# Where the group sums and the gate batches live, and the order of the first loads

## The chip, the core and the metric

The kernel runs on one core of a Trainium2 chip. Its time is the device time of one launch in microseconds; the time before is the median of 15 runs, 952.01 us (951.11 to 956.47). Engines are called as the profile calls them: PE multiplies matrices, DVE and ACT work on vectors, POOL and SP here do little but start transfers.

## What is computed

A linear attention block without softmax, with an RMS norm, feeds a two-layer MLP whose gate is h * erf(softplus(h)):

```python
kv = np.einsum('bhsd,bhse->bhde', k, v)            # q, k, v: 8 x 8 x 576 x 64, float32
out = np.einsum('bhsd,bhde->bhse', q, kv)
rms = np.sqrt(np.mean(out * out, axis=-1, keepdims=True) + 1e-06)
x = out / rms * g_norm                             # then heads side by side: 4608 x 512
h = x @ w_in                                       # w_in 512 x 2048, w_out 2048 x 512, float64
sp = np.maximum(h, 0.0) + np.log1p(np.exp(-np.abs(h)))
y = (h * erf(sp)) @ w_out                          # 4608 x 512
```

## The kernel before, in words

**Groups and batches.** The 4608 tokens are nine groups T of 512: the first 512 tokens of each of the 8 sequences, and a ninth group of their last 64 tokens each. Within a group the 2048 features are 16 chunks f of 128, in batches of 4. Attention works on pairs p of heads, four to a group: `products` (k-transposed times v, and transposes of q), `apply`, `mean` and `norm` make one quarter of a group's input x.

**Weights.** They arrive as float64. `load_w` brings raw words, `w_split` and `w_join` rebuild float32 from exponent and mantissa on DVE and ACT. During group 1 they are also cut into three reduced-precision parts (`w_upper`, `w_lower`) and written back to DRAM, from where `load_parts` fetches them over and over for groups 2 to 8.

**Groups 0 and 1** (the loop over n, L666 to L763) compute mostly with plain float32 matmuls (h_ps L713, o_ps L534). The sums over features stay in four PSUM banks o_ps and are copied out by `sums` (L553). For group 1 this is done after 12 of its 16 chunks; its last batch goes on into the main loop.

**The main loop** (m from 8 to 36, L808 to L881) does a batch per turn. `hidden` makes n_ps and m_ps for each of 4 chunks (8 and 4 matmuls); ACT copies n_ps into h (L856), DVE adds m_ps (L459), ACT takes softplus (L858) and erf (L862), DVE multiplies (L876). Then `result` multiplies the batch before, m - 1, with w_out for four token blocks j and adds into the sums e: for a group's first batch DVE writes e (L797), later it adds (L454), each time followed by the add of m_ps (L459). In a group's last batch each block is stored (L545) as soon as it is summed. So the stores of group 1 are issued in m = 8, and the first sums of group 2 are written in m = 9; the stores of group 2 come in m = 12, the first sums of group 3 in m = 13. Pieces of attention for the next group are put between.

**Tiles.** The pool `wide` (L90) has two buffers of 128 x 4 x 512 floats under one tag, taken in turns: by x of group 0, x of group 1, x_high and x_both (parts of group 1's x), the sums of group 1, and then by h of each batch from m = 8 on. So h of m = 8 follows x_both, and h of m = 9 follows the sums of group 1. The pool `acc` (L672) has one such buffer: the sums of group 0, then `old_h` (h of group 1's last batch, m = 7), then the sums of each group from 2 on (L795). An instruction that writes a reused buffer waits for the last users of the tile before it, stores among them.

**The start.** `load_part` (L120) loads one of q, k, v of a pair: q has 128 partitions with pieces of 256 bytes (256 KB), k and v 96 partitions with 1536 bytes (288 KB each). A list written by hand (L157 to L168) names, in the order of issue, the loads of pairs 0 to 2 and the engine whose queue takes each (SP or ACT). The last 64 tokens of q (`load_last`, 32 KB a pair) go over POOL, after it has made the identity and cleared bd_kv, followed by g_norm. Then SP issues two raw weight loads and pair 3, then more weights and pairs 4 and 5. The hardware queues share eight completion semaphores, so an issue waits for the landing of the eighth issue before it. `keep_warm` (L582) issues matmuls whose result nobody reads: 8 before the first pair and 4 after the first pair's products. The order of all instructions is as written (`manual_schedule`).

Of the kernel before, what the change touches and what calls it, by code (L numbers as in the profile page):

```python
# [39 lines left out]
FP32 = mybir.dt.float32  # L40
FP32R = mybir.dt.float32r
# [9 lines left out]
BATCH = 4  # L51
# [3 lines left out]
FIRST = 2  # L55
# [5 lines left out]
def kernel(  # L61
# [25 lines left out]
    attp = ctx.enter_context(tc.tile_pool(name="attp", bufs=1))  # L87
    dram = ctx.enter_context(tc.tile_pool(name="dram", bufs=1, space=bass.MemoryType.DRAM))

    wide = ctx.enter_context(tc.tile_pool(name="wide", bufs=2, side="right"))  # L90

    room, early_room, low_room = (ctx.enter_context(ExitStack()) for _ in range(3))
    first_w = room.enter_context(tc.tile_pool(name="first_w", bufs=1, side="right"))
# [23 lines left out]

        return 6 if T == 0 else 5

    def load_part(i, name, side=nc.sync):  # L120
        T, p = divmod(i, NP)
        pool = early if i in (2, 3) else kvp
        if name == "q":
            t = q_sb[T, p] = pool.tile([P, J, 2, D], FP32, name="q_sb", tag="q")
            side.dma_start(
                out=t, in_=q[T, 2 * p : 2 * p + 2, 0:G, :].rearrange("h (p j) d -> p j h d", j=J)
            )
        else:
            got, src = (k_sb, k) if name == "k" else (v_sb, v)
            C = chunks(T)  # L130
            rows, rest = divmod(S, C)
            assert rest < 2
            t = got[T, p] = pool.tile([rows + rest, 2, C, D], FP32, name=f"{name}_sb", tag=name)
            heads = src[T, 2 * p : 2 * p + 2]
            side.dma_start(
                out=t[:rows].rearrange("r h c d -> r h (c d)"),
                in_=heads[:, : S - rest].rearrange("h (r c) d -> r h (c d)", c=C),
            )
            if rest:
                side.dma_start(  # L140
                    out=t[rows:, :, 0], in_=heads[:, S - rest :].rearrange("h r d -> r h d")
                )

    def load_pair(i):
        if i < B * NP:
            for name in "qkv":
                load_part(i, name)

    def load_last(T, p, side=nc.sync):
        if T < B:  # L150
            side.dma_start(
                out=q_last[p % 2 * R : p % 2 * R + R, p // 2],
                in_=q[T, 2 * p : 2 * p + 2, G:S, :].rearrange("h r d -> r h d"),
            )


    for i, name, side in (  # L157
        (0, "k", nc.sync),
        (0, "v", nc.scalar),
        (0, "q", nc.sync),  # L160
        (1, "k", nc.scalar),
        (1, "v", nc.scalar),
        (1, "q", nc.sync),
        (2, "k", nc.sync),
        (2, "v", nc.sync),
        (2, "q", nc.sync),
    ):
        load_part(i, name, side)  # L168

    w_in_sb = first_w.tile([P, KC, DF], FP32, name="w_in_sb")  # L170
    w_out_sb = first_w.tile([P, FC, DM], FP32, name="w_out_sb")
# [1 line left out]

    ident = const.tile([P, P], FP32, name="ident")
    make_identity(nc, ident)
    bd_kv = const.tile([P, 2, P], FP32, name="bd_kv")
    nc.gpsimd.memset(bd_kv, 0.0)
    for i in range(NP):
        load_last(0, i, nc.gpsimd)
    g_col = const.tile([P, 1], FP32, name="g_col")  # L180
    for i in range(2):
        nc.gpsimd.dma_start(
            out=g_col[i * D : i * D + D, :], in_=g_norm.rearrange("(d one) -> d one", one=1)
        )
    mean_w = const.tile([P, P], FP32R, name="mean_w")
    mean_f = early.tile([P, P], FP32, name="mean_f", bufs=1)
    nc.vector.memset(mean_f, 0.0)
# [4 lines left out]
    nc.vector.memset(exp_col, -896.0 * (1 << 23))  # L192
    eps_col = const.tile([P, 1], FP32, name="eps_col")
    nc.vector.memset(eps_col, EPS)
    gm_col = const.tile([P, 1], FP32, name="gm_col")
    nc.gpsimd.tensor_scalar(out=gm_col, in0=g_col, scalar1=-0.5, scalar2=None, op0=ALU.mult)
    x_last = const.tile([P, KC, G], FP32, name="x_last")
# [85 lines left out]
    def attention(T, p, pools=None):  # L283
# [94 lines left out]
        def norm():  # L378
            ms, u, r = (st.pop(name) for name in ("ms", "u", "r"))
            nc.vector.scalar_tensor_tensor(  # L380
                out=u, in0=ms, scalar=EPS, in1=u, op0=ALU.add, op1=ALU.mult
            )
            nc.vector.scalar_tensor_tensor(
                out=u, in0=u, scalar=3.0, in1=r, op0=ALU.subtract, op1=ALU.mult
            )
            if T < FIRST:
                if T not in xT:
                    xT[T] = wide.tile([P, KC, G], FP32, name="xT", tag="h")
                x = xT[T][:, p, :]
            else:  # L390
                x = st["x"] = x_new.tile([P, G], FP32, name="x", tag="x")
            nc.vector.scalar_tensor_tensor(
                out=x,
                in0=st.pop("o"),
                scalar=gm_col,
                in1=u,
                op0=ALU.mult,
                op1=ALU.mult,
            )
# [166 lines left out]

    for _ in range(2):
        w_next("load")
    load_pair(NP - 1)

    w_rounds = {
# [4 lines left out]
        6: ("split", "join", "load", "join", "load"),  # L576
    }
    banks_0 = {"kv_ps": (ps_at, "at"), "qt_ps": (ps_h, "h"), "ms_ps": (ps_h, "h")}

    idle = ps_o.tile([P, P], FP32, name="idle", tag="o3")  # L580

    def keep_warm(n):  # L582
        for _ in range(n):
            nc.tensor.matmul(idle, lhsT=mean_w.bitcast(FP32), rhs=mean_f, start=True, stop=True)

    keep_warm(8)
    first = [attention(0, p, banks_0 | {"se_ps": (ps_o, f"o{p}")}) for p in range(NP)]
    for i in range(NP + 3):
        for piece, p in ((0, i), (1, i - 1), (4, i - 3), (3, i - 2)):
            if 0 <= p < NP:  # L590
                first[p][piece]()
        if i == 0:
            keep_warm(4)
        if i == 1:
            for _ in range(RAW - 2):
                w_next("load")
            load_pair(NP)
            load_pair(NP + 1)
        for what in w_rounds.get(i, ()):
            w_next(what)  # L600
# [65 lines left out]
    for n in range(FIRST * FC + 1):  # L666
# [23 lines left out]
            gates(done)  # L690
        if T == FIRST - 1:
            if f == 0:
                x_high = wide.tile([P, KC, G], FP32R, name="x_high", tag="h")
                x_low = low.tile([P, KC, G], FP32R, name="x_low")
                for i in range(0, KC, 2):
                    upper(xT[T][:, i : i + 2], x_high[:, i : i + 2])
                for i in range(0, KC, 2):
                    lower_only(xT[T][:, i : i + 2], x_high[:, i : i + 2], x_low[:, i : i + 2])
# [21 lines left out]
        if T < FIRST:  # L720
            if n == whole:
                old_h = acc.tile([P, BATCH, G], FP32, name="h", tag="e")
            h = hs[n] = old_h[:, n - whole] if n >= whole else unit("h_sb")
            s = ss[n] = unit("s_sb")
            if n in plain:
                nc.scalar.copy(h, plain.pop(n))
            else:
                nc.scalar.activation(h, n_ps, AF.Copy, scale=SHIFT - 1.0)
                add(h, m_ps)
            if T == FIRST - 1:  # L730
                if f == 1:
                    x_both = wide.tile([P, KC, G], FP32R, name="x_both", tag="h")
                    for i in range(0, KC, 2):
                        both_only(x_high[:, i : i + 2], x_low[:, i : i + 2], x_both[:, i : i + 2])
                    x_forms[T] = x_high, x_low, x_both
                gates(done)
                for key in list(w_new):
                    w_lower(*key)
                for key in to_cut[f]:
                    w_upper(*key)  # L740
            nc.scalar.activation(s, h, AF.Softplus)
            if n == 0:
                w_next("split")
            for piece in steps[f][1]:
                piece()
            if f % BATCH == BATCH - 1:
                for i in range(n - BATCH + 1, n + 1):
                    nc.scalar.activation(ss[i], ss[i], AF.Erf)
                softplus_table()
            if T == FIRST - 1:  # L750
                load_parts("in", {FC - 3: 2, FC - 2: 1, FC - 1: 1}.get(f, 0))
        if n >= LAG:
            T2, f2 = divmod(n - LAG, FC)
            last = n - LAG in (FC - 1, whole - 1)
            project(f2, hs[n - LAG], last)
            if last:
                sums(*((acc, "e") if T2 < FIRST - 1 else (wide, "h")))
                if T2 == 0:
                    for j in range(J):
                        store(T2, j, es.pop(j))  # L760
# [26 lines left out]
    def result(T, b, j, g, w):  # L787
# [4 lines left out]
        )  # L792
        if b == 0:
            if j == 0:
                all_e = acc.tile([P, J, DM], FP32, name="e", tag="e")  # L795
                es.update((i, all_e[:, i]) for i in range(J))
            nc.vector.tensor_scalar(  # L797
                out=es[j], in0=ps[0], scalar1=SHIFT - 1.0, scalar2=None, op0=ALU.mult
            )
        else:  # L800
            add_scaled(es[j], ps[0], SHIFT - 1.0)
# [6 lines left out]
    for m in range(first_batch, batches + 1):  # L808
# [32 lines left out]
        g, done = g_next, len(g_next)  # L841
        g_next = []
        if m < batches:
            h = wide.tile([P, BATCH, G], FP32, name="h", tag="h")
            s = gate_r.tile([P, BATCH, G], FP32, name="s", tag="s")
        for i in range(BATCH):
            if m < batches:
# [68 lines left out]
```

## Time and profile before

| | |
|---|---|
| median of 15 runs | 952.01 us |
| the profiled execution | 952.87 us, span 951.1 |
| PE busy | 932.0 us, 98% of the span |
| DVE, ACT busy | 740.9 and 616.9 us |
| DMA queues, share of 16 engines | 77.6% for SP's, 0.5% for ACT's, under 0.1% for POOL's |
| groups 0 and 1, until m = 8 begins | 255.3 us |
| 112 h copies (L856), mean | 587 ns |
| 28 first writes of sums (L797), median | 684 ns |

Times in the trace count from the start of the span. A matmul of float32 operands shows as two rows; one row of 128 x 512 in the main loop comes every 0.227 us. "Idle before" is time in which an engine had nothing running before a group of instructions, with what ended it.

### The profile page before, as it was taken

What the parts mean: (1) busy time and instruction counts of PE and PEld (TensorE: products, weight loads), DVE (VectorE), ACT (ScalarE), POOL (GpSimd) and SP (SyncE); (2) the same over time, 40 slices, a digit from 0 to 9 for tenths busy, and PEclk for the clock granted to TensorE, in tenths of its full rate; (3) what the DMA queues carried; (4) which work ended last, traced back from release to release, by engine and by line L of the source; (5) the groups of instructions that cost most, each with busy time, mean ns of one, the idle gap of its engine ahead of it and who ended that gap; (6) DMA issues with size and microseconds to landing.
All of it is one profiled execution on the core that took longest, in us unless ns stands there. A gap on an engine that the chain in (4) does not pass through costs nothing.

```text
span 951.1 us, 11799 instructions
## 1 busy us (share of the span) xinstructions
PE 932.0 (98%) x4296; PEld 687.8 (72%) x4296; DVE 740.9 (78%) x1054; ACT 616.9 (65%) x825; POOL 4.7 (0%) x14
## 2 busy tenths in 40 slices
PE   7999999999998999999999999999999999999998
PEld 5444445666686888888888888888888888878886
DVE  3979958887575888887888888888887877777667
ACT  4889876777765666666666666666666666665552
POOL 1000000000000000000000000000000000000000
PEclk9999999999999999999999999999999999999999
DMA  9856505899698888998889888988896778758872
GB/s 260 288 162 213 161 2 222 312 356 337 223 362 327 291 286 277 301 309 288 295 306 311 295 293 309 316 300 293 292 326 258 264 255 350 287 221 319 323 272 64
DMA packets 111394, 259.78 MB, mean 273 GB/s; under 512 B 43352, under 2 KB 69032, under 8 KB 111336
## 3 DMA queue, kind: packets, MB, share of 16 engines
q1 hardware_dynamic: 110200, 257.48, 77.6%
q10 hardware_dynamic: 944, 1.41, 0.5%
q8 instruction: 34, 0.56, 0.2%
q14 instruction: 24, 0.20, 0.1%
q0 software_dynamic: 192, 0.13, 0.0%
HBM read 224.40 MB, written 34.60 MB: 272 GB/s over the span
## 4 chain that ended last, share of the span: by engine, by line
PE 84%; ACT 6%; DVE 6%; DMA 2%; issue 1%; SPq 0%; DVEq 0%; ACTq 0%
PE n_ps L476 44%; PE m_ps L476 22%; PE o_ps L534 8%; PE h_ps L713 3%; PE se_ps L339 2%; PE kv_ps L311 2%; PE qt_ps L333 2%; DMA q_sb<-in_q_dram 1%; DMA w_in_parts<-w_in 1%; ACT w_e L229 1%; ACT L103 1%; DVE h L459 1%; DMA v_sb<-in_v_dram 1%; ACT w_m L233 1%; PE ms_ps L360 1%
## 5 line engine op out<-in xcount | busy, mean ns | idle before, releaser
L476 PE MATMUL n_ps<-x_forms,w_in_parts 128*128 128x512 f32 x896 | 234.3, 403 | 3.4 <-ACT h L856 1.8
L476 PE MATMUL n_ps<-w_out_parts,g_forms 128*128 128x512 f32 x928 | 231.3, 391 | 0.0
L476 PEld LDWEIGHTS n_ps<-x_forms,w_in_parts 128*128 128x128 f32 x896 | 167.7, 189 | 47.7 <-issue 9.6
L476 PEld LDWEIGHTS n_ps<-w_out_parts,g_forms 128*128 128x128 f32 x928 | 174.2, 188 | 38.4 <-issue 1.7
L858 ACT ACTIVATE s<-h 128x512 f32<-128x512 f32 x112 | 71.2, 636 | 180.9 <-DVE h L459 180.9
L459 DVE TENSOR_TENSOR h<-m_ps,h 128x512 f32<-128x512 f32 x116 | 79.9, 689 | 66.7 <-ACT h L856 48.5
L476 PE MATMUL m_ps<-w_out_parts,g_forms 128*128 128x512 f32 x464 | 124.2, 389 | 0.0
L476 PE MATMUL m_ps<-x_forms,w_in_parts 128*128 128x512 f32 x448 | 120.4, 391 | 0.0
L534 PE MATMUL o_ps<-w_out_sb,h_sb 128*128 128x512 f32 x224 | 100.8, 593 | 0.3 <-DVE h_sb L664 0.3
L476 PEld LDWEIGHTS m_ps<-w_out_parts,g_forms 128*128 128x128 f32 x464 | 87.1, 188 | 18.1
L476 PEld LDWEIGHTS m_ps<-x_forms,w_in_parts 128*128 128x128 f32 x448 | 84.2, 188 | 17.7
L459 DVE TENSOR_TENSOR e<-m_ps,e 128x512 f32<-128x512 f32 x116 | 80.3, 692 | 18.2 <-PE m_ps L476 10.9
L454 DVE SCALAR_TENSOR_TENSOR e<-n_ps,e 128x512 f32<-128x512 f32 x88 | 60.4, 686 | 38.5 <-PE n_ps L476 38.5
L534 PEld LDWEIGHTS o_ps<-w_out_sb,h_sb 128*128 128x128 f32 x224 | 42.3, 190 | 48.9 <-issue 46.6
L856 ACT ACTIVATE h<-n_ps 128x512 f32<-128x512 f32 x112 | 65.7, 587 | 11.8 <-DMA w_in_parts<-w_in 7.9
L425 DVE SCALAR_TENSOR_TENSOR g_forms<-g_forms 128x1024 fp32r<-128x1024 f32 x58 | 71.1, 1225 | 2.0
L422 DVE TENSOR_TENSOR g_forms<-h,g_forms 128x1024 fp32r<-128x1024 f32 x58 | 70.6, 1218 | 1.8 <-ACT g_forms L419 1.4
L419 ACT ACTIVATE g_forms<-h 128x1024 fp32r<-128x1024 f32 x58 | 58.9, 1061 | 13.8 <-PE m_ps L476 11.1
L876 DVE TENSOR_TENSOR h<-h,s 128x1024 f32<-128x1024 f32 x56 | 66.0, 1219 | 0.4 <-ACT s L862 0.4
L713 PE MATMUL h_ps<-xT,w_in_sb 128*128 128x512 f32 x144 | 64.9, 594 | 0.8 <-DVE w_in_sb L254 0.7
L106 ACT ACT_TABLE_LOAD x44 | 56.5, 1283 | 0.7
L862 ACT ACTIVATE s<-s 128x1024 f32<-128x1024 f32 x56 | 56.3, 1054 | 0.3
(101 smaller groups left out, 1024.4 us busy)
## 6 DMA issues: line engine op xcount, KB each, us to landing
w_out_parts<-w_out SPq DMA_DIRECT2D x116, 768.0 KB
w_in_parts<-w_in SPq DMA_DIRECT2D x112, 768.0 KB
w_in<-w_new SPq DMA_DIRECT2D x16, 768.0 KB
q_sb<-in_q_dram SPq DMA_DIRECT2D x32, 256.0 KB
w_raw<-in_moe_w_out_dram SPq DMA_DIRECT2D x8, 1024.0 KB
out_dram<-e SPq DMA_DIRECT2D x32, 256.0 KB
k_sb<-in_k_dram SPq DMA_DIRECT2D x28, 287.5 KB
v_sb<-in_v_dram SPq DMA_DIRECT2D x28, 287.5 KB
```

What stands on the lines that cost most here:

```text
L106: nc.scalar.preload_act_table_set("softplus")
L419: nc.scalar.activation(high, x, AF.Copy, scale=1.0 + 2.0**-13)
L422: nc.vector.tensor_tensor(out=low, in0=x, in1=high.bitcast(FP32), op=ALU.subtract)
L425: nc.vector.scalar_tensor_tensor(out=both, in0=low.bitcast(FP32), scalar=SHIFT, in1=high.bitcast(FP32), op0=ALU.mult, op1=ALU.add,)
L454: nc.vector.scalar_tensor_tensor(out=out_, in0=ps, scalar=scale, in1=out_, op0=ALU.mult, op1=ALU.add)
L459: nc.vector.tensor_tensor(out=out_, in0=ps, in1=out_, op=ALU.add)
L476: nc.tensor.matmul(ps, lhsT=weights(form, k), rhs=moving(form, k), start=(form == forms[0] and k == 0), stop=(form == forms[-1] and k == 3),)
L534: nc.tensor.matmul(o_ps[j], lhsT=g[:, j * P : j * P + P], rhs=w_out_sb[:, f, :], start=(f == 0), stop=last,)
L713: nc.tensor.matmul(plain[i], lhsT=w_in_sb[:, c, i % FC * P : i % FC * P + P], rhs=xT[T][:, c, :], start=(c == 0), stop=(c == KC - 1),)
L856: nc.scalar.activation(h[:, i], n_ps, AF.Copy, scale=SHIFT - 1.0)
L858: nc.scalar.activation(s[:, i], h[:, i], AF.Softplus)
L876: nc.vector.tensor_tensor(out=part(h, half), in0=part(h, half), in1=part(s, half), op=ALU.mult)
```

## The change

The group sums and the h tiles change places, and the start goes over to another order of loads without idle matmuls.

- `wide` has one buffer for each of two tags, "a" and "b". x of group 0, x_high and the sums of groups 1 to 8 take "a"; x of group 1, x_both and h of even batches m take "b"; h of odd batches takes the buffer of `acc` that the sums had.
- The loads of the start are issued pair by pair, all q on SP, k and v of pairs 0 to 2 on ACT. The last-token loads of group 0 go to SP as well: pairs 0 and 1 after the first q, pairs 2 and 3 after the first two raw weight loads. g_norm is POOL's first work.
- `keep_warm` and its PSUM tile are gone.

```diff
-    wide = ctx.enter_context(tc.tile_pool(name="wide", bufs=2, side="right"))
+    wide = ctx.enter_context(tc.tile_pool(name="wide", bufs=1, side="right"))
...
-    for i, name, side in (
-        (0, "k", nc.sync),
-        (0, "v", nc.scalar),
-        (0, "q", nc.sync),
-        (1, "k", nc.scalar),
-        (1, "v", nc.scalar),
-        (1, "q", nc.sync),
-        (2, "k", nc.sync),
-        (2, "v", nc.sync),
-        (2, "q", nc.sync),
-    ):
-        load_part(i, name, side)
...
-    for i in range(NP):
-        load_last(0, i, nc.gpsimd)
     g_col = const.tile([P, 1], FP32, name="g_col")
     for i in range(2):
         nc.gpsimd.dma_start(
             out=g_col[i * D : i * D + D, :], in_=g_norm.rearrange("(d one) -> d one", one=1)
         )
+    for i in range(NP - 1):
+        load_pair(i)
+        if i == 0:
+            load_last(0, 0)
+            load_last(0, 1)
...
+        side = nc.scalar if i < 3 else nc.sync
...
-                    xT[T] = wide.tile([P, KC, G], FP32, name="xT", tag="h")
+                    xT[T] = wide.tile([P, KC, G], FP32, name="xT", tag="ab"[T])
...
     for _ in range(2):
         w_next("load")
+    load_last(0, 2)
+    load_last(0, 3)
     load_pair(NP - 1)
...
-    keep_warm(8)
...
-        if i == 0:
-            keep_warm(4)
...
-                x_high = wide.tile([P, KC, G], FP32R, name="x_high", tag="h")
+                x_high = wide.tile([P, KC, G], FP32R, name="x_high", tag="a")
...
-                    x_both = wide.tile([P, KC, G], FP32R, name="x_both", tag="h")
+                    x_both = wide.tile([P, KC, G], FP32R, name="x_both", tag="b")
...
-                sums(*((acc, "e") if T2 < FIRST - 1 else (wide, "h")))
+                sums(*((acc, "e") if T2 < FIRST - 1 else (wide, "a")))
...
-                all_e = acc.tile([P, J, DM], FP32, name="e", tag="e")
+                all_e = wide.tile([P, J, DM], FP32, name="e", tag="a")
...
-            h = wide.tile([P, BATCH, G], FP32, name="h", tag="h")
+            pool, tag = (acc, "e") if m % 2 else (wide, "b")
+            h = pool.tile([P, BATCH, G], FP32, name="h", tag=tag)
```

In the new `load_pair` the q load of a pair always goes to SP, and `side` is the queue of its k and v.

## The prediction

> **What bounds the kernel now.** I read the page's busy shares first, then its chain of work that ended last, then the list of waits.
>
> ```profile
> PE 932.0 (98%) x4296; PEld 687.8 (72%) x4296; DVE 740.9 (78%) x1054; ACT 616.9 (65%) x825; POOL 4.7 (0%) x14
> ...
> PE 84%; ACT 6%; DVE 6%; DMA 2%; issue 1%; SPq 0%; DVEq 0%; ACTq 0%
> ```
>
> PE is busy nearly all the time and makes 84% of the chain. So only places where PE stands can be won, and a delay counts only where it makes PE stand. The list of waits (engine, line, what it waited for: total us, times, longest) has one long wait behind a DMA:
>
> ```profile
> ACT h L856 <- DMA w_in_parts<-w_in: 7.9, 1, 7.9
> ...
> PE n_ps L476 <- ACT h L856: 1.8, 1, 1.8
> ```
>
> It occurs once. What it costs is read from busy times by stretch, each stretch one batch of the main loop, cut where PE takes up n_ps<-x_forms for the next (batches m = 8 to 13; columns: length, then PE, PEld, DVE, ACT busy):
>
> ```profile
> 255.26:280.00 24.74, 24.74 (x130) 19.98 (x128) 18.67 (x28) 16.84 (x23) 0.00 (x0) 1.00 0.90 321
> 280.00:309.28 29.28, 25.93 (x130) 19.95 (x128) 19.10 (x27) 15.84 (x21) 0.00 (x0) 1.00 0.92 342
> 309.28:333.98 24.70, 24.70 (x130) 19.99 (x128) 20.16 (x30) 16.06 (x22) 0.00 (x0) 1.00 0.83 287
> 333.98:358.80 24.82, 24.82 (x131) 20.09 (x128) 20.13 (x30) 16.01 (x22) 0.00 (x0) 1.00 0.86 291
> 358.80:383.53 24.73, 24.73 (x130) 19.98 (x128) 20.28 (x30) 15.93 (x21) 0.00 (x0) 1.00 0.82 276
> 383.53:408.36 24.83, 24.83 (x131) 20.10 (x129) 20.34 (x30) 15.94 (x21) 0.00 (x0) 1.00 0.94 325
> ```
>
> Every batch takes 24.7 to 24.8 us but the second, m = 9, with 29.28. Its twin one group later is m = 13: same place in its group, same loads, 24.83. So the wait costs 29.28 - 24.83 = 4.45 us, more than PE's own 1.8, because ACT and DVE come out of it late and PE then waits for them again. The timeline shows what released ACT:
>
> ```profile
> 281.42 0.38 SPq L545 DMA_DIRECT2D out_dram<-e  x1
> ...
> 290.69 0.60 ACT L856 ACTIVATE h<-n_ps 128x512 f32<-128x512 f32 x1 [7.91 <-DMA w_in_parts<-w_in]
> ```
>
> The releaser's name is that of a load landing at the same moment. In the program the h of m = 9 takes the tile that held group 1's sums, so its first copy waits for the four stores of them; the last was issued at 281.42 and its semaphore is complete at 290.17.
>
> **The change, part by part.** The built programs' instruction orders agree on every engine but in two places: the first loads with the idle matmuls, and which waits stand in batch m = 9. DVE's order does not change at all.
>
> *The tiles.* In m = 9 ACT's first h copy and DVE's first h add lose the wait for the four stores (h now takes the tile acc "e"). DVE's first `e<-n_ps` of that batch (L797) gains it, since the sums of group 2 take the tile from which group 1's were stored. Gain of the first: 4.45 us. Price of the second: without the stall PE reaches this result as in m = 13, whose first L797 starts 397.65 - 383.53 = 14.12 us after its batch; for m = 9 that is 294.1, and the stores have landed at 290.17, 3.9 us before. The same wait already stands before L797 in groups 3 to 8 and costs nothing there; all idle time before this line is PE's:
>
> ```profile
> its engine sat idle before it (us, times) until:
>   PE n_ps L476: 11.8, 13
> ```
>
> So 0. If that cover were gone, DVE would stand, and behind it the add that frees m_ps, the gate products (L876) and the h adds, hence ACT and PE. What is late next in m = 9? Its w_in loads were issued at 258.64 (two), 270.63 and 274.67, the last is complete at 285.2 and PE wants it at about 289; of its w_out loads the last is complete at 289.5, wanted at about 292. Both hold by 2.5 us or more. Bounds of this part: -4.45 and, if all comes back, 0; I take -4.45, because the twin row shows the batch in its new state.
>
> *The first loads.* Before, SP issues k and q of pair 0, q of pair 1, k, v, q of pair 2; ACT issues v of pair 0 and k, v of pair 1; POOL the four last-token loads. Now SP has every q, with two last-token loads behind the first and two behind the first two w_raw loads; ACT has k and v of pairs 0 to 2, its last three issues waiting for landings of q of pair 0 and the first two last-token loads; POOL keeps g_norm's two. Pair 3 follows on SP in both. What counts is when pair 3 lands, because the chain of the start hangs there:
>
> ```profile
> 13.48 6.00 DMA v_sb<-in_v_dram
> 19.48 0.14 issue
> 19.62 0.92 PE kv_ps L311 x24
> ```
>
> From 20.57, when DVE copies that kv_ps, DVE's order is filled to 38 us almost without gap, then ACT's; so a later landing moves the whole rest one to one. An earlier one gains at most DVE's idle time before it since the first weights came at 14.62: 0.96 + 0.60 = 1.6 us. The bytes ahead of that landing are the same set in both orders: four pairs of q, k, v (3328 KB), four last-token loads (128), two w_raw (1024), about 4.6 MB; and the DMA engines are saturated, with 2.56 MB at 256 GB/s from 2 to 12 us and 2.48 MB at 331 from 12 to 19.5. Reordering moves bytes, it does not remove them. If all 4.6 MB went at 256, pair 3 would land at 2 + 17.9 = 19.9, that is +0.4; at the slowest 2 us slice, 239 GB/s, +1.7. I take +0.4, since q's small packets now share the engines with k and v for longer, as in that slower stretch. Bounds: -1.6 and +1.7. SP issues the last-token loads at some 0.7 us each (2.8 us in all) but gives k of pair 0 and k, v of pair 2 to ACT (0.40, 3.75 and 0.81 us), and v of pair 3 is issued 6.0 us ahead of its landing, so queues cover these. ACT's first copy (10.68) comes after its added issues; the landings they wait for (9.33 the latest before) come earlier now, so 0.
>
> *The idle matmuls.* 24 PE rows go, 12 matmuls. They do not delay anything (pair 0's kv_ps starts at 5.76 when v lands), but they bear on the clock. Granted clock by stretch (seventh number):
>
> ```profile
> 6.00:9.40 3.40, 0.86 (x24) 0.72 (x22) 0.00 (x0) 0.00 (x0) 0.00 (x0) 1.00 1.20 273
> 9.40:13.00 3.60, 3.53 (x27) 3.34 (x29) 0.73 (x3) 0.59 (x1) 0.22 (x1) 0.53 1.14 273
> 13.00:16.40 3.40, 3.40 (x52) 2.51 (x50) 1.50 (x6) 1.76 (x4) 0.00 (x0) 1.00 1.14 362
> 16.40:19.80 3.40, 2.46 (x16) 1.18 (x15) 3.20 (x9) 2.68 (x6) 0.00 (x0) 1.00 1.10 301
> 19.80:23.20 3.40, 3.40 (x35) 2.02 (x33) 2.33 (x7) 3.01 (x6) 0.00 (x0) 1.00 0.88 267
> ```
>
> After a stretch with PE 25% busy the clock was 0.53, after a full one 1.00. What it costs: four transposes took 1.04 us at the low clock and 0.66 at the full one, 24 kv matmuls 1.24 and 0.92, so a factor near 1.5. The path through PE from pair 3's kv_ps to pair 1's ms_ps is 19.62 to 23.33, 3.7 us; ACT's L372 (23.37) waits for it and DVE's L380 at 27.84 has 0.1 us of slack behind that. If this piece ran low for 3.4 us, 2.3 us of it would be done in them and 1.4 remain: +1.1. If PE is busy enough just before pair 3, as now, 0. I take the middle, +0.5.
>
> Here a rule speaks against the change. The Trainium skill, "TensorE: Matmul & The Clock Gate", Part 1 (the HAM clock gate), says that the array runs at half rate until one free-running window of about 3.4 us was busy; the rows above agree. By the rule alone the lost warm-up is at most half of one window, 1.7 us, and with it for my 0.5 the sum below would be -2.35; the page itself calls the count variable from run to run.
>
> **Sum.** -4.45 + 0.4 + 0.5 = -3.55 us. The profiled execution took 952.87 (span 951.1 and 1.8 around it), so 949.3 for such a run; it stands 0.86 above the median of the runs shown, 952.01, and from the median the sum gives **948.5**. With the bounds of the two start terms, -1.6 to +2.8, the likeliest case reaches from 945.9 to 950.4.
>
> **Rivals.**
> 1. *The old order of loads eats the gain.* Pair 3's v now waits for the first w_raw to land, which sits behind q of pair 2 in SP's queue. If w_raw lands at 14.5 as before and v goes out after it and q and k of pair 3, at 15.5, and again needs 6.0 us, it lands at 21.5: +2.0, with the clock's 1.1 it is +3.1, so about 950.7. For it: that chain of releases is new. Against: the queue has 3 us of other transfers in flight meanwhile.
> 2. *Slower: the same chain, with each link at the longest issue-to-landing seen*, the store's 8.75 us. w_raw issued at 9.1 lands at 17.9, v of pair 3, out at 18.9, lands at 27.7: +8.2, less 4.45, so about 956. It decides from a landing later than 19.5 + 4.45 + 1.9 = 25.8 on. Against: 8.75 belongs to a moment with several 768 KB loads ahead.
> 3. *The wait only moves:* DVE's L797 waits for the stores. Needs them 3.9 us later than now; then the gain is gone and the start's 0.9 stays: 952.9.
> 4. *Half is won:* a w_out load in m = 9 lands 2.5 us late or more, since the DMA share is 1.0 from 274 to 291, and the gain is 2.2: 950.7.
>
> **How the numbers follow.** The forecast 72%, rival 1 15%, rival 2 6%, rival 3 3%, rival 4 4%. A measurement of this kernel tells about 0.2%, 1.9 us, from no change: faster, below 950.1, is the forecast, 73% with the edge of rival 1; within 0.2% are the rest of rival 1, 3 and 4, 21%; slower is rival 2, 6%. The range 945.9 to 951.3 leaves out rivals 2 and 3, half of 1 and a little below.
>
> **What would show it.** Right: ACT's L856 loses its one long wait, the stretch of m = 9 is 24.8 us, L797 waits for PE alone, and pair 3's kv_ps starts within 18 to 21.5 us. Wrong: the first L713 (27.50 now) or the start of the main loop (255.26) later by over 2.5 us, a new DMA wait at L797, or m = 9 above 26 us.

## The result and the profile after

The changed kernel's median is 947.77 us (9 runs, 947.34 to 949.58); the kernel before, run beside it, has 952.72 (45 runs, 951.03 to 956.47). The ratio is 0.9951 (95% interval 0.9941 to 0.9961), so 4.7 us less, 3.7 to 5.6; the two medians differ by 4.95. The profiled execution took 948.48 us with a span of 946.7; the one of before had 952.87 and 951.1.

Line numbers moved: the h copy L856 is now L836, the add of m_ps L459 L445, the first write of sums L797 L775, n_ps and m_ps L476 L462, the store L545 L531, the first weight matmuls L713 L691, kv_ps L311 L297. The page's busy row of PE shows what did not change: less span, nearly the same work (24 rows of idle matmuls are gone).

```profile
PE 926.8 (98%) x4272; PEld 683.0 (72%) x4272; DVE 740.5 (78%) x1054; ACT 616.7 (65%) x825; POOL 2.4 (0%) x10
```

The batches m = 8, 9 and 10 of the changed kernel, cut as before (length, then PE, PEld, DVE, ACT and POOL busy, clock, DMA share, GB/s):

```profile
256.19:281.32 25.13, 25.04 (x130) 19.91 (x128) 18.67 (x28) 16.84 (x23) 0.00 (x0) 1.00 0.86 305
281.32:306.15 24.83, 24.83 (x131) 20.09 (x129) 20.06 (x29) 15.92 (x21) 0.00 (x0) 1.00 0.93 339
306.15:330.88 24.73, 24.73 (x130) 19.98 (x128) 19.95 (x30) 15.92 (x21) 0.00 (x0) 1.00 0.92 318
```

Batch m = 9 took 24.83 us where it took 29.28, and PE has no gap in it. Its timeline shows why: the last store of group 1 goes out at 283.03, and ACT's first h copy starts 0.97 us later, without waiting for its landing.

```profile
283.03 0.34 SPq L531 DMA_DIRECT2D out_dram<-e  x1
...
284.00 0.58 ACT L836 ACTIVATE h<-n_ps 128x512 f32<-128x512 f32 x1
...
295.44 0.69 DVE L775 TENSOR_SCALAR e<-n_ps 128x512 f32<-128x512 f32 x1 [0.57 <-PE n_ps L462]
```

The wait for the stores now stands before the third row, DVE's first write of group 2's sums. In brackets is what ended DVE's idle time there: PE, not a DMA. Over all 28 such writes the releasers are:

```profile
  PE n_ps L462: 13.7, 13
  DMA q_sb<-in_q_dram: 0.5, 1
```

The one row with a DMA is at 691.92, in batch m = 25, which begins at 677.80 and ends at 702.63: 24.83 us, so PE lost nothing by it. (The name may again stand for the stores of the group before, as in the prediction's reading of L856; the prediction had named a new DMA wait here as a sign of being wrong, and this one costs nothing.)

The start became slower. This is the changed kernel's chain of work that ended last, between 14 and 22 us (start, length, what); before, the same three links stood at 13.48, 19.48 and 19.62:

```profile
14.38 6.04 DMA v_sb<-in_v_dram
20.43 0.14 issue
20.56 0.92 PE kv_ps L297 x24
```

Marks along PE put the whole difference of the two profiled executions into five places:

| mark on PE | before, us | after, us | moved by |
|---|---|---|---|
| pair 3's kv_ps | 19.62 | 20.56 | +0.94 |
| first matmul with weights (h_ps) | 27.50 | 28.44 | +0.94 |
| m = 8 begins | 255.26 | 256.19 | +0.93 |
| m = 9 begins | 280.00 | 281.32 | +1.32 |
| m = 10 begins | 309.28 | 306.15 | -3.13 |
| last group, first mark | 844.87 | 841.83 | -3.04 |
| last group, next mark | 870.35 | 865.89 | -4.46 |

So: +0.94 at the start, +0.39 in m = 8, -4.45 in m = 9, +0.09 spread over the loop, and -1.42 near 849 us. Neither +0.39 nor -1.42 belongs to the change. In m = 8 PE's weight loading waited 0.5 us for one w_out load; the unaltered changed kernel, run again (e5_after_again), has 24.72 there. The -1.42 is the clock. Before, from 845.5 us on:

```profile
845.50:849.30 3.80, 2.30 (x10) 1.32 (x9) 3.77 (x6) 3.79 (x5) 0.00 (x0) 1.00 0.49 191
849.30:852.70 3.40, 3.40 (x10) 2.58 (x9) 3.19 (x5) 0.27 (x1) 0.00 (x0) 0.50 0.34 101
```

And the same work in the changed kernel:

```profile
842.50:846.30 3.80, 2.30 (x9) 1.34 (x8) 3.77 (x5) 3.79 (x5) 0.00 (x0) 1.00 0.54 194
846.30:849.70 3.40, 3.40 (x16) 2.57 (x15) 3.19 (x5) 0.23 (x1) 0.00 (x0) 1.00 0.55 157
```

In both PE is busy for 2.30 of 3.80 us, and then in one execution 3.4 us ran at half the clock (10 matmul rows instead of 16). In another profile of the kernel before (e11_before_look, 951.19 us, span 949.4) the clock stays at 1.00 there. Against that profile the change is worth 2.7 us, against the first 4.4. Medians and their ratio, not two profiles, are the measure of the whole.

### The profile page after: what moved, and what is told of

It reads as the page before. It is cut to its first block, busy times and chain, and to the rows that moved or that the text cites. A ratio compares the mean times of both kernels' runs of the same rounds, so it can differ in the third digit from the quotient of the medians.

```text
span 946.7 us, 11743 instructions
## 1 busy us (share of the span) xinstructions
PE 926.8 (98%) x4272; PEld 683.0 (72%) x4272; DVE 740.5 (78%) x1054; ACT 616.7 (65%) x825; POOL 2.4 (0%) x10
## 4 chain that ended last, share of the span: by engine, by line
PE 85%; DVE 5%; ACT 5%; DMA 3%; issue 1%; SPq 1%; DVEq 0%
PE n_ps L462 44%; PE m_ps L462 22%; PE o_ps L520 8%; PE h_ps L691 3%; PE se_ps L325 2%; PE kv_ps L297 2%; PE qt_ps L319 1%; DMA w_out_parts<-w_out 1%; DMA w_raw<-in_moe_w_in_dram 1%; ACT w_e L215 1%; DMA v_sb<-in_v_dram 1%; ACT w_m L219 1%; PE ms_ps L346 1%; PE ms_ps L347 1%; ACT L103 1%
## 5 line engine op out<-in xcount | busy, mean ns | idle before, releaser
L462 PE MATMUL n_ps<-x_forms,w_in_parts 128*128 128x512 f32 x896 | 233.2, 402 | 1.6 <-ACT x_forms L405 0.8
L462 PE MATMUL n_ps<-w_out_parts,g_forms 128*128 128x512 f32 x928 | 231.5, 391 | 0.1
L462 PEld LDWEIGHTS n_ps<-w_out_parts,g_forms 128*128 128x128 f32 x928 | 174.1, 188 | 38.8 <-issue 1.7
L462 PEld LDWEIGHTS n_ps<-x_forms,w_in_parts 128*128 128x128 f32 x896 | 166.7, 188 | 45.4 <-issue 9.1
L445 DVE TENSOR_TENSOR h<-m_ps,h 128x512 f32<-128x512 f32 x116 | 79.9, 688 | 61.0 <-ACT h L836 41.5
L462 PE MATMUL m_ps<-w_out_parts,g_forms 128*128 128x512 f32 x464 | 124.2, 389 | 0.0
L462 PE MATMUL m_ps<-x_forms,w_in_parts 128*128 128x512 f32 x448 | 120.0, 389 | 0.0
L462 PEld LDWEIGHTS m_ps<-w_out_parts,g_forms 128*128 128x128 f32 x464 | 87.1, 188 | 18.1
L462 PEld LDWEIGHTS m_ps<-x_forms,w_in_parts 128*128 128x128 f32 x448 | 84.1, 188 | 17.7
L445 DVE TENSOR_TENSOR e<-m_ps,e 128x512 f32<-128x512 f32 x116 | 80.3, 692 | 18.3 <-PE m_ps L462 11.1
L836 ACT ACTIVATE h<-n_ps 128x512 f32<-128x512 f32 x112 | 65.7, 586 | 3.9 <-PE n_ps L462 3.7
L856 DVE TENSOR_TENSOR h<-h,s 128x1024 f32<-128x1024 f32 x56 | 66.0, 1220 | 0.7 <-ACT s L842 0.7
L691 PE MATMUL h_ps<-xT,w_in_sb 128*128 128x512 f32 x144 | 65.0, 595 | 0.9 <-DVE w_in_sb L240 0.6
```

The costliest lines, as they stand in the source:

```text
L445: nc.vector.tensor_tensor(out=out_, in0=ps, in1=out_, op=ALU.add)
L462: nc.tensor.matmul(ps, lhsT=weights(form, k), rhs=moving(form, k), start=(form == forms[0] and k == 0), stop=(form == forms[-1] and k == 3),)
L691: nc.tensor.matmul(plain[i], lhsT=w_in_sb[:, c, i % FC * P : i % FC * P + P], rhs=xT[T][:, c, :], start=(c == 0), stop=(c == KC - 1),)
L836: nc.scalar.activation(h[:, i], n_ps, AF.Copy, scale=SHIFT - 1.0)
L856: nc.vector.tensor_tensor(out=part(h, half), in0=part(h, half), in1=part(s, half), op=ALU.mult)
```

## The experiments

The theory: the gain is the wait for the stores in m = 9 and nothing else; the start gives about 1 us of it back, through later transfers of pair 3 and a lower clock. Rivals: the gain lies elsewhere in the reuse of tiles; the loss is the idle matmuls' alone, the chain of releases behind the first w_raw, or one misplaced load. All kernels beside their results (e1 to e4 ran beside the same 17 runs of before, e5 to e8 beside another 9, e9 to e11 beside 9 more, e12 beside 17):

| kernel | median us (range) | before beside it | ratio (interval) | m = 8 begins | m = 9 took | GB/s from 2 to 19.5 us |
|---|---|---|---|---|---|---|
| before (first profile) | 952.72 (951.03-956.47) | | | 255.26 | 29.28 | 288 |
| after | 947.77 (947.34-949.58) | 952.72 | 0.9951 (0.9941-0.9961) | 256.19 | 24.83 | 267 |
| e1_tiles_only | 946.90 (946.76-948.82) | 951.60 | 0.9957 (0.9945-0.9969) | 255.13 | 24.83 | 287 |
| e2_start_only | 954.19 (952.17-955.93) | 951.60 | 1.0023 (1.0014-1.0031) | 255.64 | 30.76 | 283 |
| e3_after_idle | 947.75 (947.09-949.38) | 951.60 | 0.9958 (0.9945-0.9971) | 257.51 | 24.83 | 269 |
| e4_tiles_no_idle | 946.55 (946.42-947.26) | 951.60 | 0.9948 (0.9936-0.9960) | 254.54 | 24.83 | 296 |
| e5_after_again | 948.02 (947.38-950.14) | 952.34 | 0.9958 (0.9946-0.9971) | 256.61 | 24.83 | 270 |
| e6_last_early | 947.94 (947.43-949.99) | 952.34 | 0.9960 (0.9947-0.9972) | 255.75 | 24.83 | 273 |
| e7_k_first | 948.14 (947.82-948.48) | 952.34 | 0.9957 (0.9944-0.9969) | 256.61 | 24.83 | 284 |
| e8_gnorm_late | 948.89 (948.74-949.49) | 952.34 | 0.9965 (0.9951-0.9978) | 256.87 | 24.87 | 276 |
| e9_k_first_idle | 948.21 (947.91-948.81) | 951.71 | 0.9958 (0.9945-0.9972) | 256.09 | 24.83 | 292 |
| e10_no_store | 946.94 (946.61-947.04) | 951.71 | 0.9943 (0.9930-0.9955) | 255.03 | 24.82 | 289 |
| e11_before_look | 951.19 (one) | 951.71 | | 254.73 | 29.57 | 294 |
| e12_last_on_pool | 949.78 (949.38-951.39) | 951.62 | 0.9979 (0.9970-0.9987) | 258.12 | 24.83 | 262 |

**Each part alone.** e1_tiles_only is the kernel before with the tiles of the change (the hunks of `wide`, its tags, `all_e` and h); e2_start_only is the changed kernel with these hunks undone.

```diff
-            h = wide.tile([P, BATCH, G], FP32, name="h", tag="h")
+            pool, tag = (acc, "e") if m % 2 else (wide, "b")
+            h = pool.tile([P, BATCH, G], FP32, name="h", tag=tag)
```

> The kernel before with the tile edits alone: the loads of the start and the idle matmuls stay. My theory, that the two parts of the change add up (tiles -4.45, start about +0.95): batch m = 9 takes 24.8 us instead of 29.3, pair 3 is multiplied at 19.6 as before, and the time is 4.3 to 4.9 us below the kernel before, about 1 us below the changed kernel. Rival, that the new start itself brings some of the gain (the changed kernel gained more in its median than the tiles' 4.45 less the start's 0.95): this kernel is no faster than the changed one.

> The changed kernel with the tile edits undone: the new loads without idle matmuls, and the old tiles. Theory: m = 9 takes 29.3 us with ACT's one wait of about 8 us, the first matmul of group 0's hidden layer comes 0.9 us later than before (28.4 against 27.5), and the time is 0.6 to 1.4 us above the kernel before. Rival: at or below the kernel before.

The tiles alone bring 4.7 us by the medians (4.1 by the ratio, 3.0 to 5.2) and m = 9 at 24.83; their start is that of before. The start alone costs 2.6 us, more than the 0.6 to 1.4 expected. Its profile has 0.4 of it at the beginning of the main loop and 1.5 in m = 9, where ACT's first copy (L835 in this kernel) waits longer, here with the stores by name:

```profile
292.59 0.60 ACT L835 ACTIVATE h<-n_ps 128x512 f32<-128x512 f32 x1 [9.41 <-DMA out_dram<-e]
```

Busy times and clock of the same kernel's m = 9 and of the stretch after its stall:

```profile
280.41:311.17 30.76, 27.01 (x130) 21.20 (x129) 19.11 (x27) 15.81 (x21) 0.00 (x0) 0.94 0.94 345
...
293.50:296.90 3.40, 3.40 (x9) 2.65 (x9) 3.37 (x5) 1.12 (x2) 0.00 (x0) 0.50 0.52 163
```

The stall was followed by 3.4 us at half the clock: 9 rows instead of some 16. Against the first profile of before, PE's busy time in this batch is 1.08 us longer and its idle time 0.40. In the two profiles of before the clock stayed at 1.00 after the stall (29.28 and 29.57). The parts therefore do not add up: -4.7 and +2.6 are -2.1, and both together gave -4.3 (e5) to -4.95.

Every run has a mean granted clock. e2 and the changed kernel differ in the tiles alone; e2's twelve runs average 0.9972, the changed kernel's ten 0.9996. So with the new loads the old tiles cost clock in the unprofiled runs too, about 2.3 us of full speed (an estimate, 0.0024 of 950 us), and the medians of the two differ by 6.4 us where the stall alone made 4.45 before. Where in those runs the clock was low is not recorded.

**The stores by themselves.** e10_no_store is the kernel before, except that group 1's sums are not stored.

```diff
             if b2 == NB - 1:
-                store(T2, j, es.pop(j))
+                e = es.pop(j)
+                if T2 != FIRST - 1:
+                    store(T2, j, e)
```

> The kernel before, with its tiles and loads, but without the four stores of group 1: those 512 rows of the output are left out. If the wait for the stores' landing is the whole cost of the old tiles (theory), m = 9 takes 24.8 us and the time falls by 4.2 to 5.2 us, as with the tile edits. If the place of the tiles matters in itself, or the wait for DVE's last add into the old sums, m = 9 stays above 26 us and the gain below 3 us.

With the old tiles and no store to wait for, m = 9 is as short as with the new tiles, as its row of busy times shows:

```profile
279.77:304.59 24.82, 24.82 (x130) 20.09 (x129) 20.04 (x29) 15.92 (x21) 0.00 (x0) 1.00 0.94 343
```

Its median is 946.94, and e1's is 946.90. e10 also leaves out the stores' own transfers, but e1 keeps them and is as short. So the landing of the four stores is the price of the old assignment; within the spread of these runs nothing else in the reuse of tiles counts.

**The idle matmuls.** e3_after_idle puts them back into the changed kernel; e4_tiles_no_idle is e1 without them.

```diff
+    keep_warm(8)
     first = [attention(0, p, ...
...
+        if i == 0:
+            keep_warm(4)
```

> The changed kernel with the 12 idle matmuls put back in their two places. If the 0.94 us of the start come from the order of the transfers (theory), pair 3's v still lands at about 20.4, and the first h_ps matmul stays at 28.4, the time within 0.3 us of the changed kernel. If they come from a PE clock left low (rival), that matmul comes at 27.5 to 27.9 and the time falls by 0.5 to 0.9 us.

> The kernel before with the tile edits, its own order of loads, and without the idle matmuls. Theory (transfers decide the start): pair 3's v lands at 19.5 and the time equals that of the kernel with the tile edits alone within 0.4 us. Rival (the idle matmuls matter): the first h_ps matmul comes 0.5 to 1.1 us later than 27.5 and the time is that much longer.

They recover nothing in the changed kernel (947.75) and cost nothing to drop in the old order (946.55 against 946.90). e3's profile is of its slowest run (949.38): the first matmul with weights comes at 29.83, not at 28.4 as the theory had it. Its chain leads through the last-token loads of pairs 2 and 3, landed by 17.21, and has the low clock on its path, in spite of the idle matmuls; this se_ps takes 1.75 us where the full clock gives 0.91:

```profile
18.27 1.75 PE se_ps L325 x2
```

So the loss of the start is in the loads. e4 has the lowest median of this study: 5.0 us below before and 1.2 below e3, beside the same runs. e1 and e3, both with the idle matmuls, differ by 0.85 us, but their runs overlap. The kernel before has a lowest run of 950.97 to 951.25 in all five sets, so lowest runs of different sets may be compared to some 0.3 us: with the new tiles and the old loads they are 946.42 and 946.76, with the new tiles and the new order 947.09 or more.

A caution for reading the clock here. In the eight profiles without idle matmuls the view prints a clock of 1.00 for the whole start, but the first clock record in their traces comes only at 14 to 19 us (15.60 in the changed kernel). Before it, the 24 kv matmuls of pair 0 and those of pair 1 take 1.55 us each in the changed kernel, after it 0.92. There "low clock" is read from such durations.

**Which of the loads?** Over the stretch for which the prediction summed bytes, the changed kernel's DMA rates are (last number, GB/s):

```profile
2.00:12.00 10.00, 3.17 (x35) 2.64 (x37) 0.73 (x3) 0.59 (x2) 1.43 (x5) 1.00 1.00 246
12.00:19.50 7.50, 7.02 (x66) 4.93 (x63) 2.91 (x11) 3.12 (x6) 0.00 (x0) 1.00 1.12 295
```

With the old order, in e4_tiles_no_idle:

```profile
2.00:12.00 10.00, 4.41 (x54) 3.83 (x55) 0.77 (x4) 0.59 (x2) 3.32 (x7) 1.00 1.09 263
12.00:19.50 7.50, 6.60 (x58) 4.21 (x60) 4.83 (x14) 4.68 (x8) 0.00 (x0) 1.00 1.12 340
```

The new order moves less: by 19.5 us 4.67 MB against 5.04 MB in before's profile and 5.18 in e4. From 4 to 6 us it has a hole, 156 GB/s where before had 241. Five edits tried to find the load that makes it. e5_after_again is the changed kernel unaltered, for the spread between profiles. e6_last_early issues all four last-token loads behind the first q:

```diff
             load_last(0, 1)
+            load_last(0, 2)
+            load_last(0, 3)
...
-    load_last(0, 2)
-    load_last(0, 3)
```

> The changed kernel once more, unaltered, as the measure for its neighbours on the same chip: 947.3 to 948.5, m = 9 in 24.8 us, the transfers of 4 to 6 us of the start again below 200 GB/s (156 in its first profile, 241 to 253 with the old order), the first h_ps matmul at 28.0 to 28.6.

> The changed kernel with all four last-token loads of group 0 right behind the first q. In the changed kernel those of pair 2 were released by other landings, came at 17.3 us and held PE's pair 2 up, while v of pair 3 was released by the first raw weight's landing and came at 20.4; both met in DVE's order at 21.5. If the chain of releases costs the 0.94 us (rival 1 of the prediction), v of pair 3 is issued at about 12 instead of 14.4 and lands by 19.7, and 0.5 to 1 us is won. If the DMA engines' work does (theory: a hole at 4 to 6 us that nothing gives back), v is issued earlier but lands within 0.3 us of 20.4, and the time stays within 0.3 us of the changed kernel.

e5's chain, in the same program, is another one than in the first profile after. It leads through the last-token loads of pairs 2 and 3, the second issued on SP at 10.04, and then through DVE:

```profile
10.04 7.50 DMA q_last<-in_q_dram
17.54 0.14 issue
...
20.29 0.70 DVE w_in_sb L240
20.99 0.05 issue
21.04 0.92 PE kv_ps L297 x24
```

Pair 3's kv_ps starts 1.42 us later than before here, and the first matmul with weights comes at 28.91, outside the 28.0 to 28.6 expected. So in the new order two things are late at once, v of pair 3 and these last tokens, and which of them ends last differs between executions. That fits what follows, where no edit of one load gains, but it is not shown to be the reason.

In e6 the hole only moved, to 6 to 8 us (153 GB/s). v of pair 3, now held by SP's issue of k and not by w_raw, went out at 14.13 and landed at 20.11; the median stayed (947.94). The issue was expected at about 12 and came only 0.25 us earlier than in the changed kernel, so this run does not test what a really shorter chain of releases would give.

e7_k_first puts k of pair 0 on SP ahead of q, e8_gnorm_late moves g_norm's two loads behind POOL's clearing of bd_kv, and e9_k_first_idle is e7 with the idle matmuls:

```diff
-            side.dma_start(
+            (nc.sync if (i, name) == (0, "k") else side).dma_start(
...
+            if (i, name) == (0, "k"):
+                load_q()
```

> The changed kernel with one swap: k of pair 0 goes first on SP with q behind it, so that k and v of pair 0 share the engines first and the small packets of q come after, as before the change. If the hole at 4 to 6 us comes from q's small packets leading, these 2 us carry 230 GB/s or more again, v of pair 3 lands at 19.5 to 19.9 and 0.5 to 0.9 us is won against the changed kernel. If the hole stays, nothing is won.

> The changed kernel with g_norm's two transfers behind POOL's identity and bd_kv, as before the change. They are the only others on the engines at 4.5 to 6.5 us in the changed kernel (128 pieces of 4 bytes). If they make the hole, the stretch of 4 to 6 us carries 230 GB/s or more and 0.5 to 0.9 us is won. If the order of q and k does, nothing changes: within 0.3 us of the changed kernel.

> The changed kernel with k of pair 0 first on SP, and with the 12 idle matmuls. Alone, neither won anything: with k first the hole in the transfers went, but PE then ran pairs 0 to 2 at the low clock and its chain ended last; with idle matmuls alone the late transfers did. Theory, that the start's loss has these two causes side by side and either is enough: together they win 0.6 to 1.2 us against the changed kernel (946.7 to 947.4), pair 3 is multiplied at 19.5 to 20 and the first h_ps matmul comes at 27.4 to 27.9. Rival, that the last-token loads on SP hold pair 0 up (they ended PE's longest wait with k first): no gain, the first h_ps matmul stays after 28.2.

e7 closes the hole (235 GB/s) and starts pair 3's kv_ps at 19.87, but its chain no longer goes through that landing. It goes through slow matmuls, ahead of the first clock record at 17.43 (kv_ps takes 0.92 and se_ps 0.91 us at the full clock):

```profile
11.01 1.48 PE kv_ps L303 x24
...
13.86 1.81 PE se_ps L331 x2
15.67 1.48 PE kv_ps L303 x24
```

e8 was no faster (its median is 0.9 above e5's, inside e5's range), so g_norm in front is not what delays. After e7 the theory was that hole and clock stand side by side and that mending both would bring the start back. e9 has both mended, with 292 GB/s and pair 1's kv_ps in 1.00 us, and still:

```profile
14.19 6.23 DMA v_sb<-in_v_dram
20.42 0.14 issue
20.56 0.92 PE kv_ps L303 x24
```

This theory fell. v of pair 3 goes out 0.7 us later than before (13.48) and needs the same 6 us; the bytes that moved meanwhile were others'. k of pair 3 landed at 17.96 (18.18 before), but v came 2.46 us behind it (1.30 before). The issue of v moves with the order as a whole: 13.05 to 13.65 in the five profiles with the old order, 13.58 to 14.74 in the nine with the new one or a variant. No run issued pair 3 ahead of the raw weights, or on ACT, so an order in which v goes out earlier was not tried.

Last, e12_last_on_pool gives the four last-token loads back to POOL, as they were before, and leaves the rest of the new order:

```diff
-            load_last(0, 0)
-            load_last(0, 1)
...
     nc.gpsimd.memset(bd_kv, 0.0)
+    for i in range(NP):
+        load_last(0, i, nc.gpsimd)
```

> The changed kernel, but with group 0's four last-token loads issued by POOL behind its clearing of bd_kv, as in the kernel before; every other load stays where the change put it, and no idle matmuls. Theory: the start is late because these four loads stand in SP's queue, where each issue takes some 0.7 us and a place among the hardware queues' shared semaphores; then v of pair 3 is issued at 13.7 us or earlier (14.38 in the changed kernel), lands by 19.7, pair 3's kv_ps starts by 19.8 and about 0.9 us come back, so a median of 946.9 (946.4 to 947.3). Rival: what makes the start late is the order of q, k and v themselves; then v of pair 3 is issued after 14.0 or lands after 20.2 all the same, and the median is 947.8 (947.4 to 948.3).

Not the theory, and of the rival only the late landing: v of pair 3 went out at 13.98, pair 3's kv_ps started at 22.28, and the median, 949.78, is some 2 us above the changed kernel's. Its chain names the place, a 32 KB load of the last tokens, the second of the four that POOL issues behind g_norm, at 3.90 us:

```profile
3.90 8.88 DMA q_last<-in_q_dram
```

PE stands from 8.33 to 12.91 us for it, and slow matmuls follow on the chain (se_ps 1.81). Before, the same loads went out from 1.49 us on and landed by 10.08. The last-token loads are wanted early, and in the new order around them neither queue that was tried gave them a good place.

e11_before_look is one more profile of the kernel before:

> The kernel before, unaltered, for a second profile. The stall of m = 9 again makes 29.2 us or more. If the stall can cost a stretch of half clock as well (theory; the new loads with the old tiles showed 30.8 with the clock at half from 293.6 to 297.0), it is 29.3 when the clock stays full after the stall and 30.5 to 31 when it does not; the first h_ps matmul comes at 27.5. Rival: always 29.3, and 30.8 belongs to the new loads.

Its m = 9 took 29.57 us, at full clock throughout, so it leaves its rival standing: the half clock after the stall was seen in a profile with the new loads only. Its main loop begins at 254.73, which with e1, e4 and e10 makes 254.5 to 255.3 for the old order in five profiles. The new order and its variants have 255.6 to 258.1 in nine.

## Why the prediction was right, and where it was off

- **The tiles, -4.45.** Right in mechanism and size in the profiles: m = 9 fell from 29.28 to 24.83, the length of the twin batch m = 13. The new cover held too. DVE's first write starts at 295.44, 14.12 us after its batch, the distance read from the twin, and waits for PE. e1 and e10 show this alone.
- **The first loads, +0.4.** The term was mis-sized: v of pair 3 landed 0.95 later (20.43 for 19.48), inside its bounds of -1.6 and +1.7. Of this, 0.90 is a later issue (14.38 for 13.48) and 0.04 a longer transfer. The step that failed is the sum of bytes. It took the DMA engines as saturated, but their share was 0.62 from 4 to 6 us, and by 19.5 us 0.37 MB fewer had moved than before. It also took the bytes ahead of the landing as the same 4.6 MB in both orders, but before had moved 5.04 MB when v landed. That the missing bytes are the cause is not shown: e9 moved 292 GB/s, more than before's 288, and v landed at 20.42.
- **The idle matmuls, +0.5.** The profile after has none of it on the path: from pair 3's kv_ps on, the clock is 1.00 and the 24 matmuls take 0.92. Without them the slow matmuls last longer at the start (kv_ps 1.55 until the first clock record at 15.60), but that lies ahead of the wait for pair 3. The low clock was on the chain in other profiles, with the idle matmuls (e3) and without (e2, e7). Leaving them out cost nothing: e1 and e4 differ by 0.35 us, with e4, which has none, ahead. The factor of 1.5 was too small, since the 1.24 us it rests on were only partly at the low clock; 1.55 for 0.92 is 1.7, and 1.81 for 0.91 is 2. The Trainium skill, "TensorE: Matmul & The Clock Gate", Part 1 (the HAM clock gate), calls the window free-running and the number of slow matmuls variable from run to run; the rows near 849 us, equal work with clock 0.50 and 1.00, agree. By its rule up to 1.7 us, an estimate, had stood against the change; e4 shows nothing of that.
- **The sum, -3.55.** The start's two terms made +0.9 and measured +0.94, but that agreement is luck: one term measured twice its size, the other nothing, and in e5's profile the first matmul with weights is 1.41 later. The profiled executions differ by -4.39; the other -0.84 is +0.39 in m = 8, +0.09 in the loop, -1.42 of clock near 849 us, and 0.1 of start and end. The profile taken as base held a half-clock stretch that belonged to no step, and the prediction did not look for one.
- **The medians.** 947.77 lies 0.7 below 948.5. The ratio puts the gain at 4.7 where 3.5 was forecast. That the stall sometimes drew a half-clock stretch after it, as in e2's 30.76, would make its removal worth more than 4.45 on average. With the new loads the mean clocks speak for it (0.9972 and 0.9996); with the old ones they say less (0.9972 for the nine runs of before beside e10, 0.9984 for e10's five, 0.9972 for e1's five), and it is not shown there.
- **The rivals.** Rival 1's chain is there (w_raw lands at 14.37, and v goes out at 14.38), but v went out right behind that landing and not at 15.5, so it cost 0.9 and not 2. Rival 2 needed 8.75 us a link from 9.1 on; w_raw took 10.03, but went out at 4.34, and v took 6.04. Rivals 3 and 4 did not occur: DVE waits for PE in m = 9, and no weight load was late there.

What stays open is why the new order of loads fills the DMA engines less, and why v of pair 3 lands after 20 us in e9, where it fills them. Shown is that the order as a whole costs about 1 us (e4 and the changed kernel, same tiles and both without idle matmuls: 946.55 and 947.77, and their runs do not overlap), and that the loss does not come back with the idle matmuls, with g_norm moved, with the hole closed, or with the last-token loads moved up on SP or over to POOL. The chain of releases is not excluded.

## What to carry to other kernels

When a tile is reused after a store, ask which instruction waits for the landing and how much PE work stands ahead of it: here the same wait cost 4.45 us at the head of a batch and nothing 14 us into it, and a twin batch one group later gave the price to 0.01 us in these two profiles (in e11 the stall made 4.74). Judge each half of a two-part change by itself, since a good half can hide a bad one: the old order of loads with the new tiles (e4) has a lower median than both kernels. When two loads are late together, moving one of them may show nothing; look which load ends the chain in a second profile of the same program. Before a profile serves as the base of a sum, look along its granted clock for half-clock stretches, for they come and go between executions.

## What the runs showed of the hardware

- After a stretch with PE busy 2.30 of 3.80 us the clock was 0.50 for 3.4 us in one execution and 1.00 in another; it cost 1.42 us.
- A stall of PE can be followed by half clock: in e2's m = 9 PE was idle for 3.75 us and the next 3.4 us ran at 0.50, 30.76 us in all; before, with 3.35 us idle and no such stretch, the batch took 29.28.
- The profile's clock can read 1.00 where no clock was recorded: without idle matmuls the first record is at 14 to 19 us, and before it 24 kv matmuls take 1.55 us instead of 0.92.
- From issue to landing, v of pair 3 took 5.8 to 6.2 us in every kernel whose chain led through it; a 32 KB last-token load took 6.6 to 7.1 us before, 7.4 in e3, 7.5 in e5 and 8.88 in e12.
- The same loads in another order moved at 262 to 292 GB/s over the first 19.5 us, against 287 to 296 in the old order.
